# Left table factor of a long-convolution kernel: three products in one VectorE instruction, sums on TensorE

## The chip, the cores and the metric

The kernel runs on one core of one Trainium2 chip. The core has engines with a queue of instructions each, run in order: TensorE (PE, with its weight loads shown as PEld), VectorE (DVE), ScalarE (ACT), GpSimd (POOL) and SyncE (SP, which here only issues DMAs). [...] The metric is the device time of one execution in microseconds (us); lower is better.

## The reference, cut to what matters

Two branches read the same input `x` of 2048 positions by 512 channels, and a gate mixes them:

```python
g = _sigmoid((x * gate_w).sum(-1, keepdims=True))
a = _A_ref(x, A_re, A_im, B_re, B_im, C_re, C_im, log_dt, Dskip)
b = _B_ref(x, wqkv, w_phi, wo)
return g * a + (1 - g) * b
...
# _A_ref: a long convolution per channel d, by FFT
logdA = dt * A;  dB = dt * Bc                                  # complex, (512, 128)
P = jnp.exp(logdA[:, :, None] * l[None, None, :])              # l = 0..2047
K = jnp.einsum("dn,dnl,dn->dl", Cc, P, dB).real                # the convolution's kernel
y = irfft2(rfft2(pad(u)) * rfft2(pad(K)))[..., :L] + u * Dskip
...
# _B_ref: linear attention, 32 heads of 16
phi_k = concat(softmax(k @ w_phi), softmax(-k @ w_phi));  phi_q likewise
num = phi_q @ (phi_k^T v);  den = phi_q . sum(phi_k) + 1e-6;  o = (num / den) @ wo
```

What the change touches is `K`: for each channel a sum over 128 complex modes of C times dB times an exponential in the position `l`, of which the real part is kept.

## The kernel before, in words

**The table for K.** The 128 modes lie on the partitions. A position is split as l = 512a + 64b + t, with a in 0..3, b in 0..7 and 64 values of t. So the exponential is a product of three: the left factor is A(a,b) = C(a) times D(b), 32 complex values for each mode and channel, where the table `Ctab` (C) holds the term in a with C and dB folded in, and `Dtab` (D) holds the term in b; the right factor R(t) is made of a real exponential (`E`, stretched by `Gtab`) times a cosine and a sine (`cs`). K is the real part, so it is the sum over modes of Re(A) Re(R) and Im(A) Im(R) with signs put into the tables; TensorE does that sum with A as the 32 columns of weights and R as 64 moving columns, once per channel.

**Units.** The 512 channels go in 16 units U of 32. Units 0 to 7 take their C from the first half of the table (`C[0]`), 8 to 15 from the second (`C[1]`). In `kgen` each unit has on DVE: `A1` (L1037), which multiplies two planes of C by the first plane of D; `A2` (L1042), which multiplies two planes of C by the second plane of D (C has three planes, the third being the negative of the first); and for six units `A3` (L1047), which adds the two results. Each of these instructions writes 2048 bf16 values per partition. The table `FOURS` says for which ten units A3 is left out: TensorE then adds the four products itself (`kgen_chunk`, L209: four terms of 32 matmuls, 128 in all; with A3 two terms, 64 matmuls). `El` (L989), `Rh` (L1054) and `Rl` (L1058) make R. There is one buffer for A, so A1 of the next unit waits until the matmuls of this one are done.

**Stages.** Until about 99 us (`prepare`, `keys_and_spectrum`, `attention_keys`): loads, transposes of x, the forward transform of x (`XAu`, `xst`, written to `XUd`), the tables C, D, G, and the keys and values of the attention. There ACT makes exponentials of the keys (`Ek`), DVE sums them (`Zk`), and values are copied out of PSUM into one of two buffers `vb` and scaled (`vr`, L692). Then the units follow each other. Behind every four of them, 128 channels are transformed (`psA`, `XA`, `psB`, `XK`), multiplied with the spectrum of x (`t`, L1230), transformed back (`psz`, `Zr`, through DRAM as `Zd` and `ZT`, `psy`), gated (`xT<-psy`, L1330) and written out (L1341). The attention's queries are worked in between. The last four units go as groups (12, 13), (14) and (15), and the last one in halves (`KD`, `KDb`; `XA`, `XAb`).

**The order.** `Plan` records every step as a node with what it needs and the buffers it takes; `ORDER`, a string of node numbers, fixes in which order they are issued; `SIDES` says for each copy out of PSUM (L175 on ACT, L177 on DVE) and for some DMA issues on which engine it goes, and `RINGS` from which ring its PSUM buffer comes. Nothing is decided while it runs. A line such as L96 (ACT functions) or L347 (`tt`, DVE products of tables) belongs to a helper; the tile's name tells the step.

Of the kernel before, what the change touches and what calls it, by code (L numbers as in the profile page):

```python
# [98 lines left out]
class Plan:  # L99

    DIGITS = "0123456789abcdefghijklmnopqrstuvwxyzABCDEFGHIJKLMNOPQRSTUVWXYZ-_"
    ORDER = ("0001021d0x0y0z0o0p0q0G0H0I0f0g0h0D0E0F170i0j0k181415162z2C0304051h2E0l0m0n0607082F0u0v0w2D0r0s0t2G2I2K1e1f090a0b1C2H0c0d"
             "0e1g2M1A1i1j1k0A0B0C1r2L2N2O2J1D1s102P11121t131L0-1E1u1v1w2S1M0_1B2Q2T2R1N1F1I0Y2U1b0Z1G2V1J191a2W0J0K0L0M0N0O0P0Q0R0S0T"
             "0U0V0W0X1c1S2X4n202Y2Z4u4v4w2A2-4x4J2_304y4K4L4M31324B4F4z4A4C1H4N344G4D334Q4E4H4I4Y1P4R364O354Z4U371K4P1R4S4-4V4_533839"
             "542B4T504W1X1O571Y4X513a525b3C585c3c5d5e59555i3b5j563d5a5f5q5r5g3h5m1U5s3i5h5t5k5x3D5n3j5o5l5u5y3e3f3g5B5p1Z5F5v5C3k5w3o"
             "5H5z5G5D5M5A5I3q1T5E215J3E3p5Q1V5R5K4o5N5L5U1Q3r3l3m3n4p1l1m1n5O1x1y1z1-5W3v3x5V5S3y5P3F1W3w5X5T67693G4q683I5Y6a3H6b3J5Z"
             "3K6c3M1o1p1q5-6d3L3N3s3t3u3O1_235_3P223Q3R25243S3U3T2b272d3V263W2c3z3A3B2f3X2h2e28632j2i3Y3Z3-3_402g2l412k43442s2u482942"
             "2t2m4a2n4b2o454647492p4f2q4c4d4e2w2r2v4h2a2x6064612y4i4g656e874r6i628b6f6j4j4k4l6g6686858a6k4m6h6l886r6m7x898c4s8d8e6t6q"
             "8h8i4t8j8f8n8g6u7y8k8l8B8o8t8p6v6w6s8C6-8m6x8q6y8u6_70718r9_8Y8Z8-8H6z8s6A6B72748v8D7z8Ia06n6o6p756C736D9293948w8K8E8F6E"
             "8L8x8y6F6G6H768M8G8z778Q787B8A7C8J6I6J6K8Ra8796M6N6O7a7A8N8Oa97b9R8P8S9Va19W6Laaa26P9S8T7D9X7c7d7e9U9Z8U6Qa5a36Sa68W8Vae"  # L110
             "a48X9Ta79Y6Tam7f7g7h9-6U6Ranaf7i6W7Eabac98as8_9091ad996X9a7F9g7Gag6V7n7H9h7Iao7j7k7lbSah7JbT7patavaw9b9i7K9596977m9c9j9k"
             "7L7M7Nap9o9paBaxbI9w9x6YaibMbNajakbJaqal6Z9q7r7O7P7QbO7S7T7U7oar7qauaC7RbL7sbQay9y7t7Waz9l9m9naA7YbK7u7vaD7ZaPaQaR7VbPb_"
# [1479 lines left out]
```

## Time and profile before

| | |
|---|---|
| Time, median of 3 runs | 252.83 us (251.02 to 253.78) |
| The profiled execution's own time | 252.17 us |
| Its span on the core | 250.4 us |
| DVE busy | 224.2 us, 90% |
| ACT busy | 211.0 us, 84% |
| PE busy | 202.3 us, 81% |
| POOL busy | 2.4 us, 1% |

A profile is one execution. "Busy" is the time in which an engine executes an instruction. A group of instructions has a count, a total and the mean of one; since the next instruction of a queue starts a little before the last one's end is recorded, the distance from start to start is the better price of an instruction in a full queue. "Idle before" names how long the engine stood still ahead of a group and what ended that. The granted clock of TensorE was 1.00 in most of the span, and 0.52 between 75 and 90 us.

### The profile page before, as it was taken

The page shows a single profiled execution, that of the slowest core. Times are in us where ns is not written, and L with a number is a line of the kernel's source. Part 1 is how long each engine was busy: PE and PEld are TensorE (multiplying, and loading weights), DVE is VectorE, ACT ScalarE, POOL GpSimd, SP SyncE. Part 2 cuts the span into 40 slices and gives each one's busy share as a digit, 9 for nine tenths or more (in the row PEclk, how much of TensorE's full clock was granted, in tenths as well). Part 3 has the DMA queues.
Part 4 walks back from the last instruction along what each step waited for, and adds up shares of the span by engine and source line. Part 5 has one row for each costly group of instructions (what it writes and reads, how often), then busy time and mean ns, then how long its engine had stood idle before and what let it go on. Part 6 is the DMA issues. An engine that isn't in the chain of part 4 may idle for free.

```text
span 250.4 us, 9850 instructions
## 1 busy us (share of the span) xinstructions
PE 202.3 (81%) x4412; PEld 141.8 (57%) x4437; DVE 224.2 (90%) x287; ACT 211.0 (84%) x291; POOL 2.4 (1%) x7
## 2 busy tenths in 40 slices
PE   0695999999956468798797778889999789998970
PEld 0584755447734434256456646765777576877550
DVE  0388999989899988999999999999999999999680
ACT  2058999999999999999999999999999999974430
POOL 0200000000000000000000000000000000000000
PEclk9999999999995569999979999999999999999985
DMA  6999910236280477400619129804896879998664
GB/s 134 275 174 159 404 49 4 90 105 134 56 256 0 145 235 223 160 3 13 174 49 240 38 73 243 265 3 92 197 209 192 219 206 234 225 235 165 185 171 75
DMA packets 61922, 38.23 MB, mean 153 GB/s; under 512 B 40632, under 2 KB 57272, under 8 KB 61496
## 3 DMA queue, kind: packets, MB, share of 16 engines
q1 hardware_dynamic: 61880, 37.61, 60.0%
q8 instruction: 34, 0.56, 1.0%
q14 instruction: 8, 0.07, 0.1%
HBM read 24.49 MB, written 13.11 MB: 150 GB/s over the span
## 4 chain that ended last, share of the span: by engine, by line
PE 28%; DVE 24%; ACT 23%; DMA 10%; SPq 7%; issue 5%; ACTq 0%; DVEq 0%
ACT Eq L96 4%; PE pk L635 4%; ACT cs L96 4%; DMA UD<-in_A_u_dram 4%; PE vp L683 4%; SPq L1465 3%; ACT E L96 3%; PE kps L209 2%; DMA ZT<-Zd 2%; PE psB L542 2%; ACT XA L175 2%; ACT L93 2%; DVE t L1230 2%; PE psy L750 2%; PE psz L1256 2%
## 5 line engine op out<-in xcount | busy, mean ns | idle before, releaser
L209 PEld LDWEIGHTS <-A 128*32 128x32 bf16 x1664 | 28.5, 160 | 6.2 <-issue 3.6
L209 PE MATMUL kps<-R,A 128*32 128x64 bf16 x1664 | 30.3, 229 | 1.8 <-DVE A L1042 0.5
L96 ACT ACTIVATE cs<-args 128x1024 bf16<-128x1024 f32 x32 | 30.7, 1050 | 0.2 <-PE args L953 0.2
L1058 DVE TENSOR_TENSOR R<-E,cs 128x2048 bf16<-128x2048 bf16 x16 | 19.5, 1217 | 0.0
L1037 DVE TENSOR_TENSOR A<-Ctab,Dtab 128x2048 bf16<-128x2048 bf16 x16 | 19.5, 1217 | 0.0
L1054 DVE TENSOR_TENSOR R<-E,cs 128x2048 bf16<-128x2048 bf16 x16 | 19.5, 1217 | 0.0
L1042 DVE TENSOR_TENSOR A<-Ctab,Dtab 128x2048 bf16<-128x2048 bf16 x16 | 19.5, 1217 | 0.0
L175 ACT CAST Zr<-psz 128x1024 bf16<-128x1024 f32 (+1 forms) x17 | 16.5, 974 | 2.5 <-issue 1.2
L542 PE MATMUL psB<-XAu,TB 64*128 64x128 bf16 x256 | 12.8, 262 | 7.1 <-ACT xst L175 4.9
L175 ACT CAST XK<-psB 128x1024 bf16<-128x1024 f32 (+1 forms) x15 | 15.0, 1010 | 3.8 <-PE psB L222 2.3
L175 ACT CAST XA<-psA 128x1024 bf16<-128x1024 f32 (+1 forms) x16 | 15.6, 1002 | 3.2 <-PE psA L216 3.2
L683 PE MATMUL vp<-WW,xT 128*128 128x512 bf16 x59 | 16.9, 403 | 0.8 <-issue 0.7
L1230 DVE TENSOR_TENSOR t<-XUX,XK 128x2048 bf16<-128x2048 bf16 x14 | 17.0, 1218 | 0.5 <-ACT XK L175 0.5
L96 ACT ACTIVATE Ek<-pk 128x512 bf16<-128x512 f32 x32 | 16.8, 602 | 0.4 <-PE pk L635 0.2
L769 PE MATMUL pq<-xT,Wqp 128*128 128x512 bf16 x64 | 16.5, 396 | 0.6 <-ACT Eq L96 0.6
L96 ACT ACTIVATE Eq<-pq 128x512 bf16<-128x512 f32 (+1 forms) x28 | 16.7, 711 | 0.2 <-PE pq L769 0.2
L96 ACT ACTIVATE E<-args 128x1024 bf16<-128x1024 f32 x16 | 16.8, 1058 | 0.0
L542 PEld LDWEIGHTS <-TB 64*128 64x128 bf16 x256 | 10.3, 116 | 11.2 <-issue 11.0
L1256 PE MATMUL psz<-t,small 128*128 128x512 bf16 x49 | 14.6, 380 | 2.0 <-ACT cs L96 0.5
L635 PE MATMUL pk<-WW,xT 128*128 128x512 bf16 x57 | 15.5, 380 | 0.5 <-issue 0.2
L662 DVE TENSOR_REDUCE Zk<-Ek 128x64 f32<-128x1024 bf16 x12 | 14.0, 1209 | 0.0
L222 PE MATMUL psB<-XA,TB 128*128 128x128 bf16 (+2 forms) x160 | 9.6, 205 | 4.1 <-ACT XA L175 1.4
(178 smaller groups left out, 463.8 us busy)
## 6 DMA issues: line engine op xcount, KB each, us to landing
...
```

The source lines that it names most:

```text
L96: return self.nc.scalar.activation(**kw)
L175: self.nc.scalar.copy(out=o, in_=i)
L209: nc.tensor.matmul(kps[32 * dj:32 * dj + 32, g4, e, :], lhsT=A[:, ka, :, :, d].rearrange("p a b -> p (a b)"), rhs=R[:, kr, d, :], start=(i ...
L542: nc.tensor.matmul(box.ps[:, c2, sl, :], lhsT=fc.TB[rows, b0:b0 + 2].rearrange("p a b -> p (a b)"), rhs=X.t[rows, k, r0 + sl].rearrange("p ...
L635: nc.tensor.matmul(box.ps[:], lhsT=xT[:, st, kt, :], rhs=g.WW[:, kt, :], start=(kt == 0), stop=(kt == 3))
L683: nc.tensor.matmul(box.ps[:], lhsT=xT[:, st, kt, :], rhs=g.WW[:, 4 + kt, :], start=(kt == 0), stop=(kt == 3))
L1037: nc.vector.tensor_tensor(out=c.A[:, 0:2].rearrange("p o a b c -> p (o a) b c"), in0=g.C[U // 8][:, 0:2, :, d0 % 256:d0 % 256 + 32].rearra ...
L1042: nc.vector.tensor_tensor(out=c.A[:, 2:4].rearrange("p o a b c -> p (o a) b c"), in0=g.C[U // 8][:, 1:3, :, d0 % 256:d0 % 256 + 32].rearra ...
L1054: nc.vector.tensor_tensor(out=c.R[:, :, :, 32:64], in0=t.E[:, 1].unsqueeze(1).to_broadcast([128, 2, 32, 32]), in1=t.cs[:], op=ALU.mult)
L1058: nc.vector.tensor_tensor(out=c.R[:, :, :, 0:32], in0=t.E[:, 0].unsqueeze(1).to_broadcast([128, 2, 32, 32]), in1=t.cs[:, ::-1, :, ::-1], o ...
L1230: nc.vector.tensor_tensor(out=box.t, in0=Ls[r0 // ns].X[:], in1=box.XK[:].unsqueeze(1).to_broadcast([128, 2, 1024]), op=ALU.mult)
L1256: nc.tensor.matmul(box.ps[:, hb, :], lhsT=fc.TI[:, k].rearrange("p h a t -> p (h a t)"), rhs=box.t[:, k, 512 * hb:512 * hb + 512], start=( ...
```

## The change

A complex product can be had from three multiplications: with C = R + iI and D = d0 + i d1 (signs aside), the products (I - R) d0, (I + R) d1 and R (d0 - d1) are enough, since the last plus the second is R d0 + I d1 and the last plus the first is I d0 - R d1. The change does this as follows.

- The C table's three planes hold R, I - R and I + R. In `prepare` the sum over both planes (one instruction of 2048) and the sign flip (`p_cn`) of each half give way to four instructions of 1024: `p_cr`, `p_ci`, `p_cm`, `p_cp`.
- `Dtab` gets five planes and is laid out unit by unit: planes 0 and 1 (channels 0 to 255) and 3 and 4 (256 to 511) are d0 and d1, plane 2 is d0 - d1, made by one instruction of 2048 (`DS0` ahead of the first unit, `DS1` ahead of unit 8).
- A unit has one DVE instruction `A1` of 3072 in place of A1, A2 and A3, and always 128 matmuls: `kgen_chunk` adds two of the three products for each part.
- The value buffers `vb`, now four, lie in plane 2 of D; DS0 therefore waits for the last `vr`. `zrow` (the gate's row) lies in columns of `TB` that the forward transform is done with, and the small `rows` have a tile of their own.
- `ORDER`, `SIDES` and `RINGS` are other strings.

```diff
@@ class Plan @@
-    ORDER = ("0001021d0x0y0z0o0p0q0G0H0I0f0g0h0D0E0F170i0j0k181415162z2C0304051h2E0l0m0n0607082F0u0v0w2D0r0s0t2G2I2K1e1f090a0b1C2H0c0d"
...
+    ORDER = ("0l0m0n0001020x0y0z1h1e1d0304050607081C1A1D0o0p0q14151f0f0g0h160i0j0k1L0r0s0t0Y171i1g1r1s1t1M181T0G0H0I0-0D0E0F090a0b0c0d"
...
-    FOURS = ("0111111101011000")
...
-def kgen_chunk(nc, kps, A, R, four):
+def kgen_chunk(nc, kps, A, R, h):
 
+    terms = ((2, 0), (2, 1), (1, 0), (0, 1)) if h == 0 else ((0, 0), (0, 1), (2, 0), (1, 1))
     for e in range(2):
         for g4 in range(4):
-            terms = [(k, k) for k in range(2)] if not four else [(0, 0), (2, 0), (1, 1), (3, 1)]
...
-                                     rhs=R[:, kr, d, :], start=(i == 0), stop=(i == len(terms) - 1), tile_position=(0, 32 * dj), skip_group_check=True)
+                                     rhs=R[:, kr, d, :], start=(i == 0), stop=(i == 3), tile_position=(0, 32 * dj), skip_group_check=True)
...
@@ def prepare @@
-        V("p_px", lambda h=h: tt(C[h][:, 0:2], F.P[:], F.Q[:], ALU.add), r="t0 t1 t5 t6", w=f"Cn{h} Ci{h}")
-        V("p_cn", lambda h=h: nc.vector.tensor_scalar(out=C[h][:, 2], in0=C[h][:, 0], scalar1=-1.0, scalar2=None, op0=ALU.mult), r=f"Cn{h}", w=f"C{h}")
+        oR, oM, oP = (2, 0, 1) if h == 0 else (0, 1, 2)
+        V("p_cr", lambda h=h, oR=oR: tt(C[h][:, oR], F.P[:, 0], F.Q[:, 0], ALU.add), r="t0 t1 t5 t6", w=f"Cn{h} Ci{h} C{h}")
+        V("p_ci", lambda: tt(F.P[:, 1], F.P[:, 1], F.Q[:, 1], ALU.add), r="t0 t1", w="t5 t6")
+        V("p_cm", lambda h=h, oM=oM, oR=oR: tt(C[h][:, oM], F.P[:, 1], C[h][:, oR], ALU.subtract), r="t5 t6", w=f"C{h} Ci{h} Cn{h}")
+        V("p_cp", lambda h=h, oP=oP, oR=oR: tt(C[h][:, oP], F.P[:, 1], C[h][:, oR], ALU.add), r="t5 t6", w=f"C{h} Ci{h} Cn{h}")
...
@@ def attention_keys @@
             def cv(box=box):
-                box.v = g.kwk.tile([128, 16, 32], BF16, name="vb", bufs=g.P.k["vb"])
+                box.k = g.vfree.pop(0)
+                box.v = g.D[:, 2, 2 * box.k:2 * box.k + 2].rearrange("p u b c -> p (u b) c")
...
+    P.add("DVE", "DS0", lambda: nc.vector.tensor_tensor(out=g.D[:, 2], in0=g.D[:, 0], in1=g.D[:, 1], op=ALU.subtract), vs + [polar], rw=("", "DS"))
...
@@ def kgen @@
             def a1(c=c, d0=d0, U=U):
-                c.A = g.wk.tile([128, 4, 4, 8, 32], BF16, name="A", tag="A", bufs=g.P.k["A"])
-                nc.vector.tensor_tensor(out=c.A[:, 0:2].rearrange("p o a b c -> p (o a) b c"),
...
-            def a2(c=c, d0=d0, U=U):
...
-            def a3(c=c):
-                nc.vector.tensor_tensor(out=c.A[:, 0:2], in0=c.A[:, 0:2], in1=c.A[:, 2:4], op=ALU.add)
...
+                c.A = g.wk.tile([128, 3, 4, 8, 32], BF16, name="A", tag="A", bufs=g.P.k["A"])
+                h, c0 = U // 8, d0 % 256
+                nc.vector.tensor_tensor(out=c.A[:], in0=g.C[h][:, :, :, c0:c0 + 32].unsqueeze(3).to_broadcast([128, 3, 4, 8, 32]),
+                                        in1=g.D[:, 2 * h:2 * h + 3, U % 8].unsqueeze(2).to_broadcast([128, 3, 4, 8, 32]), op=ALU.mult)
+
+            if U == 8:
+                P.add("DVE", "DS1", lambda: nc.vector.tensor_tensor(out=g.D[:, 2], in0=g.D[:, 3], in1=g.D[:, 4], op=ALU.subtract), [sh], rw=(Dk, "DS"))
+            an = [P.add("DVE", "A1", a1, [sh], take=["A"], rw=(Ck + " " + Dk + " DS", ""))]
...
@@ def full_kernel @@
-        P = Plan(nc, {"XAu": 1, "UDp": 1, "xst": 2, "wT": 1, "Ek": 2, "Zk": 2, "vr": 2, "vb": 2, "acc": 1, "r8": 3, ...
+        P = Plan(nc, {"XAu": 1, "UDp": 1, "xst": 2, "wT": 1, "Ek": 2, "Zk": 2, "vr": 2, "vb": 4, "acc": 1, "r8": 3, ...
...
-        g.D = persist.tile([128, 2, 8, 512], BF16, name="Dtab")
+        g.D = persist.tile([128, 5, 8, 8, 32], BF16, name="Dtab")
```

How the order of DVE's queue changes where the units begin: before, from the attention's `KVbd` on (`zrow` and `SSw` belong to the gate and the attention, `zs` and `den` to its queries).

```order
L718 TENSOR_TENSOR KVbd<-kvp,small 32x8x32 x4
L721 TENSOR_TENSOR SSw<-small,zcol 128x8x8
L1037 TENSOR_TENSOR A<-Ctab_72,Dtab 128x2048
L1042 TENSOR_TENSOR A<-Ctab_72,Dtab 128x2048
L620 TENSOR_SCALAR zrow<-zps 128x512
L1047 TENSOR_TENSOR A<-A 128x2048
L989 TENSOR_TENSOR E<-E,Gtab 128x1024
L1054 TENSOR_TENSOR R<-E,cs 128x64x32
L1058 TENSOR_TENSOR R<-E,cs 128x64x32
```

And the same place of DVE's queue in the changed kernel (L734 is `DS0`, L1048 the wide A1).

```order
L726 TENSOR_TENSOR KVbd<-kvp,small 32x8x32 x4
L729 TENSOR_TENSOR SSw<-small,zcol 128x8x8
L734 TENSOR_TENSOR Dtab<-Dtab 128x2048
L1048 TENSOR_TENSOR A<-Ctab_71,Dtab 128x3072
L1057 TENSOR_TENSOR R<-E,cs 128x64x32
L1000 TENSOR_TENSOR E<-E,Gtab 128x1024
L1061 TENSOR_TENSOR R<-E,cs 128x64x32
```

DS0 has come in front of the first unit, and one instruction stands where three stood.

The end of DVE's queue before, from the copy of the last unit's K on (`KD`, L177; L1281 is a transpose of 32 by 32 blocks, L1330 the gating of a convolution's result, L913 that of the attention's alone):

```order
L177 CAST KD<-kps 128x256
L177 CAST KDb<-kps 128x256
L177 CAST xT<-bps 128x2x128
L177 CAST XAb<-psA 128x512
L1233 TENSOR_TENSOR t<-XUX,XK 128x2x512 x2
L177 CAST xT<-bps 128x2x128
L177 CAST XK<-psB 128x512
L1168 TENSOR_TENSOR t<-XUX,XK 128x2x512
L913 TENSOR_SCALAR xT<-bps,gT 128x384
L1168 TENSOR_TENSOR t<-XUX,XK 128x2x512
L1281 STREAM_TRANSPOSE ZS<-Zr 128x1024
L1330 TENSOR_TENSOR xT<-psy,gT 128x16x64
```

The same end of DVE's queue in the changed kernel (L1333 and L1331 are the gatings, L1284 the transpose):

```order
L175 CAST KD<-kps 128x256
L175 CAST KDb<-kps 128x256
L175 CAST XA<-psA 128x512
L1236 TENSOR_TENSOR t<-XUX,XK 128x2x512
L1333 TENSOR_TENSOR xT<-psy,gT 128x8x128
L1236 TENSOR_TENSOR t<-XUX,XK 128x2x512
L1171 TENSOR_TENSOR t<-XUX,XK 128x2x512
L1331 TENSOR_TENSOR xT<-psy,gT 128x4x128
L1171 TENSOR_TENSOR t<-XUX,XK 128x2x512
L175 CAST Zr<-psz 128x1024
L175 CAST Zr<-psz 128x32x16
L1284 STREAM_TRANSPOSE ZS<-Zr 128x1024
```

Behind these rows follow a third copy of `Zr` (128x32x16), a transpose and the four gatings of the last channels, the one of 16x64 now as the last of them, where it was the first. The gatings of 8x128 and 4x128, which stood just ahead of the KD rows before, now stand behind them; the three copies of `Zr` were ACT's; the copies of `bps` and one of `XK` have gone to ACT.

The end of SP's queue before, which holds only DMA issues:

```order
L1341 DMA out_dram<-xT 32x12x128 x2
L1290 DMA ZT<-Zd_0_118 32x2048 x4
L1341 DMA out_dram<-xT 32x12x128 x2
L1341 DMA out_dram<-xT 32x12x256 x4
L925 DMA out_dram<-xT 32x4x384 x4
L1341 DMA out_dram<-xT 512x1x64 x8
```

The end of ACT's queue in the changed kernel, which now holds the last eight writes (L1344), behind its last copies and gatings:

```order
L173 CAST xT<-bps 128x2x128
L922 ACTIVATE xT<-bps,gT 128x384 x2
L173 CAST xT<-bps 128x2x128
L922 ACTIVATE xT<-bps,gT 128x384
L1344 DMA out_dram<-xT 512x1x64 x8
```

SP's queue there ends with the four writes of 32x4x384, and the eight have moved from SP to ACT.

More of the change, by code (lines that the diff above doesn't have):

```diff
@@ L362, in prepare @@
     for b in range(8):
-        S("p_d", lambda b=b: act(out=g.D[:, 0, b, :], in_=are(), func=ACT.Exp, scale=64.0 * (b - 3.5)), r="act t2", w=f"D{b}")
+        S("p_d", lambda b=b: act(out=g.D[:, 0:4:3, :, b, :], in_=are().rearrange("p (h u c) -> p h u c", h=2, u=8), func=ACT.Exp, scale=64.0 * (b - 3.5)), r="act t2", w=f"D{b}")
     S("p_g", lambda: act(out=g.G[:], in_=are().unsqueeze(2).to_broadcast([128, 512, 2]), func=ACT.Exp, scale=-32.0), r="act t2", w="G")
@@ L619, in ge @@
     def ge():
-        nc.vector.tensor_scalar(out=g.zrow[:], in0=G.ps[:], scalar1=80.0, scalar2=-80.0, op0=ALU.min, op1=ALU.max)
+        nc.vector.tensor_scalar(out=g.zrow, in0=G.ps[:].rearrange("p b (k t) -> p b k t", k=4), scalar1=80.0, scalar2=-80.0, op0=ALU.min, op1=ALU.max)
         G.ps = None
     a2 = P.add("PE", "zps", gd, [b] + xt, take=["ps"], rw=("atm", ""))
-    g.gate.append(P.add("DVE", "g_z", ge, [a2], drop=["psum"]))
+    g.gate.append(P.add("DVE", "g_z", ge, [a2], drop=["psum"], rw=("", "TB0")))
     g.xTr = [a, a2]
-    kv = []
+    kv, vs, g.vfree = [], [], list(range(P.k["vb"]))
     for s2 in range(8):
@@ L805, in z2 @@
             nc.vector.tensor_tensor(out=Q.den[:, 0, :], in0=Q.den[:, 0, :], in1=Q.den[:, 1, :], op=ALU.add)
-            nc.vector.tensor_tensor(out=Q.z[:, 0:2, :], in0=Q.z[:, 0:2, :], in1=g.zrow[:, b:b + 1, :].to_broadcast([128, 2, 128]), op=ALU.add)
+            zk = Q.z[:, 0:2, :].rearrange("p s (k t) -> p s k t", k=4)
+            nc.vector.tensor_tensor(out=zk, in0=zk, in1=g.zrow[:, b].unsqueeze(1).to_broadcast([128, 2, 4, 32]), op=ALU.add)
         def z3():
@@ L1030, in kgen @@
             plan_exp(P, nc, g, psum, U, t, psq, [sh])
-            four = P.FOURS[U] == "1"
             c = Bag()
@@ L1401, in full_kernel @@
         g, fc, at = Bag(), Bag(), Bag()
[L1402 removed]
+        P = Plan(nc, {"XAu": 1, "UDp": 1, "xst": 2, "wT": 1, "Ek": 2, "Zk": 2, "vr": 2, "vb": 4, "acc": 1, "r8": 3, "ax": 1, "nrm": 1, "E": 2, "cs": 4, "A": 1, "R": 2,
                       "KD": 1, "XA0": 1, "XK": 2, "Zr": 2, "XUX": 3, "ln": 8}, {"ps": 2, "p0": 2, "bk": 3, "acc": 1, "pf": 2})
@@ L1437, in full_kernel @@
         g.ldc, g.gw, g.Dcol_b = g.vecs[:, 0:4], g.vecs[:, 4:8], g.vecs[:, 8:12]
-        g.rows = g.zrow[0:12, 0, 0:64].bitcast(BF16)
         ck = ExitStack()
@@ L1453, in full_kernel @@
         g.wc = g.up.tile([128, 4, 16], BF16, name="wc")
+        g.rows_t = g.up.tile([128, 128], BF16, name="rows")
+        g.rows = g.rows_t[0:12]
         g.oT = {}
@@ L1493, in shift @@
         def shift():
-            g.rawd = g.ld_b = g.up = g.xau = g.ptmp = g.wc = None
+            g.rows_t = g.rows = g.rawd = g.ld_b = g.up = g.xau = g.ptmp = g.wc = None
             cu.close()
```

78 lines of the change are left out of this document (36 added, 42 removed).

## The prediction

> **What bounds the kernel now.** I read the page's totals first, then the chain that ended last, and then windows of the trace cut where the kernel's stages change, because a mean over 250 us mixes stages with different limits.
>
> ```profile
> span 250.4 us, 9850 instructions
> ...
> PE 202.3 (81%) x4412; PEld 141.8 (57%) x4437; DVE 224.2 (90%) x287; ACT 211.0 (84%) x291; POOL 2.4 (1%) x7
> ...
> PE 28%; DVE 24%; ACT 23%; DMA 10%; SPq 7%; issue 5%; ACTq 0%; DVEq 0%
> ```
>
> No engine has the chain to itself. The windows (columns: stretch, length, then busy us and instructions of PE, PEld, DVE, ACT and POOL, granted clock, DMA share, GB/s) say where each of them counts.
>
> ```profile
> 24.80:93.70 68.90, 57.87 (x915) 37.09 (x928) 65.93 (x98) 65.19 (x106) 0.00 (x0) 0.88 0.44 134
> 99.20:228.60 129.40, 113.59 (x2858) 82.27 (x2870) 128.39 (x136) 123.57 (x159) 0.00 (x0) 0.99 0.60 153
> 177.00:190.00 13.00, 12.47 (x371) 9.56 (x370) 12.97 (x17) 12.40 (x17) 0.00 (x0) 1.00 0.80 180
> 228.60:250.40 21.80, 13.38 (x373) 8.55 (x364) 12.39 (x19) 6.21 (x10) 0.00 (x0) 0.82 0.64 153
> ```
>
> The second row is the stage of the units, which is what the change is about. DVE is idle for only 1.0 of its 129.4 us, so DVE is the bound there. ACT has 5.8 us of idle and PE 15.8 us. What DVE is spared shortens the stage only until PE, which gets more work, or ACT is full. In the best 13 us (third row) PE reached 12.47/13.00 = 96%, in the whole stage 88%. The last row is the tail, where no engine is full: there a longer chain counts in full.
>
> ```profile
> 99.22 1.22 DVE L1037 TENSOR_TENSOR A<-Ctab,Dtab 128x2048 bf16<-128x2048 bf16 x1
> ...
> 230.84 0.41 DVE L177 CAST KD<-kps 128x256 bf16<-128x256 f32 x1
> ```
>
> These two instructions cut the execution in three: 99.22 us up to the first A, 230.84 - 99.22 = 131.6 us for the stage up to the copy of the last unit's K, and the rest. The profiled execution took 252.17 us, 1.77 more than its span, and is 0.66 below the median of 252.83. The sum is made on 252.17, and I do not correct for the difference, which is far inside the scatter of the three runs.
>
> **Prices.** They are taken from start to start in a full DVE queue.
>
> ```profile
> 157.06 1.22 DVE L1037 TENSOR_TENSOR A<-Ctab,Dtab 128x2048 bf16<-128x2048 bf16 x1
> 158.20 1.22 DVE L1230 TENSOR_TENSOR t<-XUX,XK 128x2048 bf16<-128x2048 bf16 x1
> ...
> 160.47 0.68 DVE L177 CAST oT<-ops 128x512 bf16<-128x512 f32 x1
> 161.07 1.22 DVE L840 TENSOR_TENSOR Eq<-Eq,ax 128x2048 bf16<-128x2048 bf16 x1
> ...
> 163.93 0.68 DVE L989 TENSOR_TENSOR E<-E,Gtab 128x1024 bf16<-128x1024 bf16 x1
> 164.54 1.22 DVE L1037 TENSOR_TENSOR A<-Ctab,Dtab 128x2048 bf16<-128x2048 bf16 x1
> ```
>
> A product of 2048 costs 1.14 us (157.06 to 158.20), a product of 1024 costs 0.61, and a copy of 512 out of PSUM 0.60. From 1024 to 2048 the price rises by 0.53, so an instruction of 3072 should cost 1.14 + 0.53 = 1.67 us. No row shows that size. From below it is bounded by 1.14, and from above by 3 x 1.14 = 3.4, three of the old ones; I take the straight line because two points lie on it. Copies of 1024 out of PSUM last as long as products of 2048 and are priced like them:
>
> ```profile
> L177 DVE CAST xst<-psB 128x1024 bf16<-128x1024 f32 x6 | 7.3, 1218 | 0.4 <-PE psB L542 0.4
> L175 ACT CAST xst<-psB 128x1024 bf16<-128x1024 f32 x10 | 10.0, 1024 | 1.2 <-DMA XUd<-xst 0.9 <-PE psB L542 0.3
> ```
>
> **Up to the first A: +1.5 us.** In each of two halves a sum of 2048 and a sign flip give way to four instructions of 1024.
>
> ```profile
> 84.06 0.42 DVE L386 TENSOR_SCALAR Ctab<-Ctab 128x1024 bf16<-128x1024 bf16 x1
> 84.39 1.22 DVE L347 TENSOR_TENSOR ppx<-Ctab,pt 128x2048 bf16<-128x2048 bf16 x1
> ```
>
> That is 1.14 + 0.33 before and 4 x 0.61 after, +0.97 for a half and +1.9 for both. DS0 is one more product of 2048, +1.1, and stands directly ahead of the first A, so whatever it waits for holds the whole queue of units behind it. Against that one copy of `vb` (0.6) and a few small steps (1.0 together) stand earlier in the new order, where the first row of the windows leaves DVE 3.0 and ACT 3.7 us of idle in 68.9. The sum is +1.4, taken as +1.5. If the new order hides all of it in that idle it is 0; if DS0, which must wait for every value of the attention, also has to wait for ACT, it is +3.
>
> **The stage of the units on DVE: -11.0 us.**
>
> ```profile
> L1037 DVE TENSOR_TENSOR A<-Ctab,Dtab 128x2048 bf16<-128x2048 bf16 x16 | 19.5, 1217 | 0.0
> L1042 DVE TENSOR_TENSOR A<-Ctab,Dtab 128x2048 bf16<-128x2048 bf16 x16 | 19.5, 1217 | 0.0
> L1047 DVE TENSOR_TENSOR A<-A 128x2048 bf16<-128x2048 bf16 x6 | 7.3, 1217 | 0.0
> ```
>
> 38 instructions of 1.135 are 43.1 us; 16 of 1.67 are 26.7; so -16.4. DS1 gives back 1.1. Four copies of 1024 that were ACT's (one KD, two XA, one XK) cost 4 x 1.14 = 4.5, two of 512 (one wo, one table) 1.2, and the two small steps of the gate 0.3: +6.0. The gatings of 8x128 and 4x128 have gone behind the cut, 1.1 + 0.6 = -1.7. The stage would be 131.6 - 11.0 = 120.6 us if DVE stayed the bound. ACT loses those four copies at 1.02 at least, so it needs at most 123.57 x 131.6/129.4 - 4.1 = 121.6.
>
> **The same stage on PE: -8.0 us, and this is the term I take.** Six units go from 64 to 128 matmuls.
>
> ```profile
> 112.73 2.25 PE L209 MATMUL kps<-R,A 128*32 128x64 bf16 x128
> 114.91 1.04 PE L769 MATMUL pq<-xT,Wqp 128*128 128x512 bf16 x4
> ...
> 210.06 1.21 PE L209 MATMUL kps<-R,A 128*32 128x64 bf16 x64
> 211.20 1.04 PE L1256 MATMUL psz<-t,small 128*128 128x512 bf16 x3
> ```
>
> 128 take 2.18 us (17 ns each) and 64 take 1.14, so 6 x 1.04 = +6.2, with the other 0.3 allowed for starts. [...]
>
> Work that moves behind the cut on PE: two groups of 32 `psy` matmuls, 16 products with `wo`, and one eighth of the attention's `ops`.
>
> ```profile
> L1319 PE MATMUL psy<-ZT,TJ 64*32 64x128 bf16 (+1 forms) x256 | 4.4, 211 | 0.3 <-DMA ZT<-Zd 0.3
> L750 PE MATMUL psy<-wo,oT 128*128 128x128 bf16 x96 | 7.4, 219 | 0.0
> L859 PE MATMUL ops<-Eq,KVbd 128*128 128x256 bf16 x64 | 8.5, 274 | 0.0
> ```
>
> These are 2 x 0.55 + 1.2 + 1.1 = 3.4 us. PE had 113.6 us of work in the second window and, at the same 88%, 2.0 in the 2.2 us from its end to the cut. With +6.5 and -3.4 it has 118.7 us. At the 96% of its best stretch that takes 123.6 us, more than DVE's 120.6 and ACT's 121.6. So PE, not DVE, ends the stage: 131.6 - 123.6 = 8.0 us less. The ends are -11.0 (PE's rows contain slack, DVE stays the bound) and +2.8 (PE keeps all its idle, below).
>
> **The tail: +1.8 us.** Behind the cut DVE gets the two gatings (+1.7) and three copies of `Zr`, one of 1024 and two of 512 (1.1 + 1.2), and loses two copies of 256 (0.7) and one of 512 (0.6): +2.8, all laid on the path, although it need not all be. Then come the last writes.
>
> ```profile
> 243.80 0.42 DVE L1330 TENSOR_TENSOR xT<-psy,gT 128x256 bf16<-128x256 f32 x1 [0.50 <-PE psy L1319]
> ...
> 242.50 5.35 SPq L1341 DMA_DIRECT2D out_dram<-xT  x8
> ```
>
> SP issues eight writes in 5.35 us, 0.67 each, up to 247.85, and the last lands at the span's end, 2.5 us later. From the last gating's end (244.22) to the end are 6.2 us. After the change ACT issues them; the 16x64 gating is now the last, with four issues behind it: 4 x 0.67 + 2.5 = 5.2, so -1.0. What an issue costs ACT is not shown; twice SP's price would add 2.7, and nothing excludes a gain of the same 0.67 or so for each. I take SP's price because it is the only row. The sum is +2.8 - 1.0 = +1.8, with ends -1 and +4.5.
>
> **The sum.** 252.17 + 1.5 - 8.0 + 1.8 = 247.5 us.
>
> **Rivals.** First, PE has more slack than its busy row shows, and DVE stays the bound: -11.0 for -8.0 gives 244.5. The windows speak for it in that weight loads take only 82.27 of 129.40 us, 64%; against it, that PE waited little in its full stretches. [...] Chance 0.20.
>
> Second, the ends of the table and the tail both come out high (+3 and +4), or the stage gives only about half of its 8.0 because ACT, which has up to 121.6 us of work there between the same waits, stands still meanwhile: 250 to 255. Chance 0.20.
>
> Third, slower: PE becomes the bound and keeps its idle time. A has one buffer, so the next A1 waits until all 128 matmuls of the unit before are done, and DVE's copies of PSUM are queued behind that A1; PE then waits for those copies, as it waits for ACT's now:
>
> ```profile
> L222 PE MATMUL psB<-XA,TB 128*128 128x128 bf16 (+2 forms) x160 | 9.6, 205 | 4.1 <-ACT XA L175 1.4
> L953 PE MATMUL args<-selE,statC 64*128 64x512 bf16 x32 | 6.8, 404 | 3.9 <-ACT cs L96 1.7 <-ACT E L96 1.2 <-ACT XA L175 0.5
> ```
>
> With all 15.8 us of idle the stage would be 118.7 + 15.8 = 134.5, 2.9 longer than now, and the sum 252.17 + 1.5 + 2.9 + 1.8 = 258.4. It decides from the point where PE's idle stays above 131.6 - 118.7 - 3.3 = 9.6 us. Against it: those waits end by ACT, which is relieved. Chance 0.12.
>
> Fourth, the wide instruction, whose operands have one more dimension, loses DVE's rate and costs three times 1.14 = 3.4: 16 x 1.7 = 28 more on DVE, some 273 us. Against it, another instruction that reads its operands in short runs keeps the rate:
>
> ```profile
> L1058 DVE TENSOR_TENSOR R<-E,cs 128x2048 bf16<-128x2048 bf16 x16 | 19.5, 1217 | 0.0
> ```
>
> Chance 0.03.
>
> **How the numbers follow.** The forecast has 0.45: PE at about 96% in the stage, 247.5 us. Two runs of this kernel differ by up to 1%, so about 1% is what a measurement can tell from no change; that is 250.3 to 255.4. Below it lie the first rival and nearly all of the forecast, 0.64; within it the second, 0.21; above it the third and fourth, 0.15. The range leaves out those two and a little on either side: from 243.0, the first rival with 1.5 less for table section or tail, to 254.5, nearly the end of the second.
>
> **What would show it.** The A group has 16 instructions of about 1750 ns and DVE's busy total falls to about 214 us; `kps` has 2048 matmuls. The first A starts near 100.7 us and the KD copy near 224.3. Between them PE's idle falls to about 5 us, and DVE has 3 us of idle, most of it ahead of A or a copy and ended by PE. ACT's queue issues the last eight writes. If the A group's mean is above 2 us, the price of 3072 was wrong; if the stage is near 121 us, the first rival holds; if PE's idle there is above 10 us, the third; and if the stage is right but the end is not, the table section or the tail was mis-sized.

## The result: slower by 5.1%

The changed kernel takes 265.13 us (median of 4 runs, 265.09 to 267.16) against 252.96 us of the kernel before (251.02 to 253.78). The ratio is 1.051, with a 95% interval of 1.044 to 1.059: 12 us slower, where 247.5 us were forecast. Its profiled execution took 265.09 us, with a span of 263.4 us on the core. Some executions of a kernel run longer at a lower clock (in experiment 5 three of 269.9 to 271.1 us at a mean granted clock of 0.93, against one of 265.5 at 0.94): the ratios leave them out, and since the profiled executions of experiments 5, 6 and 13 were of that kind, places in their traces are read, and no conclusion rests on their times alone.

The page of the changed kernel, the lines that answer to those of before:

```profile
span 263.4 us, 10603 instructions
...
PE 209.0 (79%) x4801; PEld 148.5 (56%) x4821; DVE 216.1 (82%) x274; ACT 208.0 (79%) x288; POOL 2.7 (1%) x7
...
ACT 40%; PE 28%; DVE 14%; issue 10%; DMA 3%; SPq 1%; ACTq 0%; DVEq 0%
```

DVE lost 8.1 us of work (about 10 were forecast), and ACT 3.0. "issue", time in which an engine waited for nothing that the profile shows, has doubled from 5% to 10% of the chain that ended last. The same cuts as in the prediction, by windows of the changed kernel (stage of the units; a hole; the rest of the tail; the last writes), and the tail of the kernel before:

```profile
99.90:230.70 130.80, 116.60 (x3202) 85.32 (x3209) 119.87 (x122) 115.86 (x149) 0.00 (x0) 0.98 0.56 145
230.70:236.10 5.40, 0.70 (x25) 0.62 (x26) 0.76 (x2) 0.00 (x0) 0.00 (x0) 0.85 0.92 149
236.10:255.40 19.30, 17.47 (x382) 12.23 (x382) 12.90 (x17) 6.45 (x11) 0.00 (x0) 0.85 0.31 75
255.40:263.40 8.00, 0.00 (x0) 0.00 (x0) 0.00 (x0) 0.00 (x0) 0.00 (x0) 0.50 0.74 168
```

```profile
230.80:244.30 13.50, 11.43 (x277) 6.87 (x277) 10.69 (x18) 4.68 (x8) 0.00 (x0) 0.94 0.67 181
```

Three things are to be seen. The stage is as long as before (130.8 for 131.6 us), although DVE has 10 us less to do: its idle time has grown from 1.5 to 11 us, and ACT's from 6.5 to 15. Then PE stands still for 4.7 of 5.4 us while the DMA engines are 92% busy, and behind that the granted clock is at half for some 5 us. And the tail behind that hole is still 19 us where it was 13.5. The clock from 236 to 241 us (the number before the DMA engines' share is their row's granted clock) and then the timelines of PE and of DVE:

```profile
236.00:241.00 5.00, 4.87 (x81) 4.46 (x81) 2.51 (x4) 1.60 (x2) 0.00 (x0) 0.50 0.50 107
```

```profile
230.61 0.79 PE L220 MATMUL psB<-XA,TB 128*128 128x32 bf16 x25
236.13 0.35 PE L220 MATMUL psB<-XA,TB 128*128 128x32 bf16 x7 [4.73 <-issue]
```

```profile
230.73 0.42 DVE L175 CAST KD<-kps 128x256 bf16<-128x256 f32 x1 [2.85 <-PE kps L207]
231.07 0.41 DVE L175 CAST KDb<-kps 128x256 bf16<-128x256 f32 x1
238.49 0.69 DVE L175 CAST XA<-psA 128x512 bf16<-128x512 f32 x1 [7.00 <-PE psA L214]
```

The wide instruction and the matmuls cost what was worked out for them (groups of the changed kernel):

```profile
L207 PE MATMUL kps<-R,A 128*32 128x64 bf16 x2048 | 36.5, 230 | 5.4 <-issue 3.6
L1048 DVE TENSOR_TENSOR A<-Ctab,Dtab 128x3072 bf16<-128x3072 bf16 x16 | 28.0, 1751 | 3.7 <-PE kps L207 3.7
```

| piece of the span | before | after | moved | forecast |
|---|---|---|---|---|
| up to the first A | 99.22 | 99.87 | +0.7 | +1.5 |
| first A to the copy of KD | 131.6 | 130.9 | -0.8 | -8.0 |
| KD to the end of the last gating | 13.4 | 24.6 | +11.2 | +2.8 |
| the last writes | 6.2 | 8.1 | +1.9 | -1.0 |
| span | 250.4 | 263.4 | +13.0 | -4.7 |

So two questions: why did the stage not get shorter, and what made the tail longer?

### The profile page after: what moved, and what is told of

It reads as the page before. It is cut to its first block, busy times and chain, and to the rows that moved or that the text cites. A ratio compares the mean times of both kernels' runs of the same rounds, so it can differ in the third digit from the quotient of the medians.

```text
span 263.4 us, 10603 instructions
## 1 busy us (share of the span) xinstructions
PE 209.0 (79%) x4801; PEld 148.5 (56%) x4821; DVE 216.1 (82%) x274; ACT 208.0 (79%) x288; POOL 2.7 (1%) x7
## 4 chain that ended last, share of the span: by engine, by line
ACT 40%; PE 28%; DVE 14%; issue 10%; DMA 3%; SPq 1%; ACTq 0%; DVEq 0%
ACT Ek L96 4%; PE kps L207 4%; ACT cs L96 4%; ACT xst L173 4%; ACT XAu L173 3%; PE pq L779 3%; PE psy L760 2%; DVE R L1057 2%; ACT trg L96 2%; ACT E L96 2%; DVE R L1061 2%; PE psz L1259 2%; PE psy L1322 2%; ACT XK L173 2%; DVE A L1048 2%
## 5 line engine op out<-in xcount | busy, mean ns | idle before, releaser
L207 PE MATMUL kps<-R,A 128*32 128x64 bf16 x2048 | 36.5, 230 | 5.4 <-issue 3.6
L207 PEld LDWEIGHTS <-A 128*32 128x32 bf16 x2048 | 34.6, 161 | 9.7 <-issue 5.9
L1048 DVE TENSOR_TENSOR A<-Ctab,Dtab 128x3072 bf16<-128x3072 bf16 x16 | 28.0, 1751 | 3.7 <-PE kps L207 3.7
L1057 DVE TENSOR_TENSOR R<-E,cs 128x2048 bf16<-128x2048 bf16 x16 | 19.4, 1218 | 1.4 <-ACT E L96 1.4
L1061 DVE TENSOR_TENSOR R<-E,cs 128x2048 bf16<-128x2048 bf16 x16 | 19.4, 1219 | 0.2
L688 PE MATMUL vp<-WW,xT 128*128 128x512 bf16 x61 | 15.8, 392 | 0.5 <-issue 0.5
L547 PE MATMUL psB<-XAu,TB 64*128 64x128 bf16 x256 | 11.2, 244 | 5.3 <-ACT xst L173 2.7
L173 ACT CAST Zr<-psz 128x1024 bf16<-128x1024 f32 x14 | 14.2, 1044 | 1.4 <-PE psz L1259 1.2
L173 ACT CAST XA<-psA 128x1024 bf16<-128x1024 f32 x13 | 13.1, 1032 | 2.0 <-PE psA L214 1.9
L640 PE MATMUL pk<-WW,xT 128*128 128x512 bf16 x57 | 14.3, 379 | 0.5 <-issue 0.2
L547 PEld LDWEIGHTS <-TB 64*128 64x128 bf16 x256 | 9.3, 108 | 8.9 <-issue 8.9
L173 ACT CAST xst<-psB 128x1024 bf16<-128x1024 f32 x14 | 14.0, 1030 | 0.2 <-PE psB L547 0.2
```

The lines of the kernel that those rows point to most:

```text
L173: self.nc.scalar.copy(out=o, in_=i)
L207: nc.tensor.matmul(kps[32 * dj:32 * dj + 32, g4, e, :], lhsT=A[:, ka, :, :, d].rearrange("p a b -> p (a b)"), rhs=R[:, kr, d, :], start=(i ...
L547: nc.tensor.matmul(box.ps[:, c2, sl, :], lhsT=fc.TB[rows, b0:b0 + 2].rearrange("p a b -> p (a b)"), rhs=X.t[rows, k, r0 + sl].rearrange("p ...
L640: nc.tensor.matmul(box.ps[:], lhsT=xT[:, st, kt, :], rhs=g.WW[:, kt, :], start=(kt == 0), stop=(kt == 3))
L688: nc.tensor.matmul(box.ps[:], lhsT=xT[:, st, kt, :], rhs=g.WW[:, 4 + kt, :], start=(kt == 0), stop=(kt == 3))
L1048: nc.vector.tensor_tensor(out=c.A[:], in0=g.C[h][:, :, :, c0:c0 + 32].unsqueeze(3).to_broadcast([128, 3, 4, 8, 32]), in1=g.D[:, 2 * h:2 * ...
```

## The experiments

Every kernel is cut at its own first A and KD. "Stage" is the length from the first A to KD in its profiled execution, and "tail" the length from KD to the end of the last gating; the expectations count some tails to the end of the span, with the last writes.

**1. The arithmetic in the old order.** The changed kernel with `ORDER`, `SIDES` and `RINGS` of the kernel before:

```
-    ORDER = ("0l0m0n0001020x0y0z1h1e1d...      # as changed
+    ORDER = (the nodes in the order of the kernel before; A1 where A1 was; p_cr, p_ci, p_cm, p_cp where p_px was; DS0, DS1 ahead of A1 of units 0 and 8)
```

> The changed arithmetic (wide A1, five-plane D, new C tables, always 128 matmuls) in the issue order, engine sides and PSUM rings of the kernel before; the wide A1 stands where A1 stood, A2 and A3 are gone, DS0 and DS1 stand directly ahead of the first A1 that needs them. PE theory (TensorE with its waits has become the bound of the stage of the units, whatever the order): the stage stays at 129 to 134 us, and with the tail of the kernel before the time is 251 to 256 us. Order theory (the new order loses what the arithmetic gains): the stage falls to 121 to 126 us and the time to 243 to 249 us. Either way the tail behind the copy of KD is back at 18 to 21 us from 32.7.

Measured: 264.82 us, ratio 1.054 [1.045, 1.062]. The tail is back at 14.7 us (20.2 with the last writes, as expected), but the stage has grown to 141.9 us, 10 more than before. Neither theory had that. The new order alone is thus not what costs the 12 us: with the old one the same arithmetic costs as much, in another place.

**2. The last inverse transforms behind the last unit.** On PE `psy` of the third quarter goes behind `psB` and `psz` of the last unit (`psBh` and `opsL` are the halves of its `psB` and the last `ops`, `pya` is the attention's part of `psy`):

```
 psA psBh opsL psBh psz      # the last unit
+psy128 pya psy128           # third quarter, stood ahead of psA (first) and behind opsL, psBh
```

> The changed kernel with one thing in its order moved: on TensorE the two inverse transforms (psy) of the third quarter of the channels, which need the last load of ZT but one, stand behind the transforms of the last unit's K (psA, psB, psz) instead of ahead of them; their gatings on VectorE and their writes follow. Theory of the tail (TensorE's 4.7 us standstill at 231.4 us is the wait for that load, and everything of the last unit queues behind it): 4 to 6 us less than the changed kernel, 259 to 261 us. Rival (the tail is set by the DMA traffic, the Zd and ZT transfers and the last writes, and the standstill only fills time): less than 1 us of change, 264 to 266 us.

Measured: 267.67 us, ratio 1.069, slower still. The hole was not the wait for that load: `psA` stands right behind `psB` now, and the hole is there all the same, 3.9 us at the same matmul.

```profile
229.90 0.79 PE L220 MATMUL psB<-XA,TB 128*128 128x32 bf16 x25
234.61 0.35 PE L220 MATMUL psB<-XA,TB 128*128 128x32 bf16 x7 [3.92 <-issue]
```

My theory of the tail fell with this, and I looked for what these standstills have in common. In several kernels they lie a multiple of 256 PE instructions apart, matmuls and weight loads counted alike (in the changed kernel 767, 2045, 1276 and 510 recorded instructions lie between the standstills that end at 138.1, 157.7, 196.9, 222.9 and 236.1 us, which is 3, 8, 5 and 2 times 256 less one to four, and a trace can lack a few records); and the trace has packets on an instruction queue of its own (queue, packets, MB, share of the DMA engines' time; the page of the changed kernel):

```profile
q8 instruction: 37, 0.61, 1.0%
```

These are 16 KB each, and PE's 9622 matmuls and weight loads on 37 packets are 260 a packet, as are the 8849 on 34 packets of the kernel before. From here on the theory is: PE's program comes in pages of 256 instructions, and PE stands still where it has run through a page before the next has arrived.

**3. More matmuls, less VectorE, in the kernel before.**

```
-    FOURS = ("0111111101011000")
+    FOURS = ("1111111111111111")
```

> The kernel before with the table FOURS all ones: the six A3 additions are gone from VectorE (6 x 1.14 = 6.8 us) and six units go from 64 to 128 matmuls on TensorE (+6.5 us), in the order of the kernel before. Theory that VectorE bounds the stage and TensorE's idle time can be filled: 4 to 7 us faster, 246 to 249 us. PE theory (TensorE with its waits is as much the bound): within 2 us of the kernel before, 251 to 255 us, with VectorE idle by 4 to 7 us more.

Measured: 265.4 us, ratio 1.055 [1.050, 1.060]. One string in the kernel before, which takes 6.8 us from DVE and adds 6.5 us to PE by the prices of the prediction, gives a loss of the same size. It lies in the stage, 143.2 us, where that of the changed kernel lies in the tail. So in the old order what matters is the 384 additional matmuls, and their price is near twice their time.

**4. Half of the products on TensorE.** In the changed kernel:

```
-            for i, (ka, kr) in enumerate(terms):
+            for i, (ka, kr) in enumerate(terms[:2]):
```

> The changed kernel with only two of the four products of each part of K computed on TensorE (64 matmuls for a unit instead of 128, 1024 fewer, 17 us); the other two are left out, so K is not complete. PE theory: the stage from the first A to the copy of KD falls by 6 to 11 us from 130.8, to where VectorE is full (120 to 125 us). Rival (the stage is held by waits of the order between ScalarE and VectorE, not by TensorE's work): it stays above 128 us. The tail keeps its standstill.

Measured: 258.24 us (one run). The stage is 128.1 us, only 2.8 less, for 17 us less matmul time by the price of one (11 us less busy time). The hole in `psB` is gone, against what was expected: PE stands still for 1.1 us at a later place (236 us), and the tail is 18.9 us.

**5. The whole program shifted by half a page.**

```
                 box.ps = psum([128, 4, 256], "psA")
+                for i in range(64 if h == 1 and g4 == 7 else 0):
+                    nc.tensor.matmul(box.ps[0:32, 0, 0:64], lhsT=..., rhs=..., start=True, stop=True, ...)
```

> The changed kernel with 64 additional small matmuls (32 weight columns, 64 moving columns, 128 instructions with their weight loads, about 1.1 us) on TensorE in an idle stretch at about 73.4 us, where they write PSUM that the next matmuls overwrite. They only shift everything behind them by half of 256 instructions in TensorE's program. Fetch theory (TensorE stands still at every 256th instruction when the next 16 KB of its program has not arrived): at the five places where it stood still without a named cause (138.1, 157.7, 196.9, 222.9 and 231.4 us, 10.0 us together) it runs through, and the standstills, if any, come 64 matmuls earlier or later; the time changes by more than 1.5 us in either direction from 265.1. Rival (these standstills are waits for data that the profile does not name): the same five places, about 10 us together, and 265 to 266.5 us.

Measured: 270.31 us median, 265.49 to 271.14, without a ratio. Only places are read from it: `psB` of the last unit runs through, and PE stands still in other places, all half a page from the old ones: at 183, 192, 198 and 232 us, and for 2.5 us up to 239 us, between the 89th and the 90th of the last unit's 128 matmuls. The hole has moved, and is not gone.

**6. The last writes on SyncE again.**

```
 # SIDES of the four "out" nodes of the last channels
-ACT
+SP
```

> The changed kernel with its last eight output writes issued by SyncE again instead of ScalarE; nothing else. Theory (SyncE's remaining writes stood from 247.96 to 255.79 us because they waited for a write that ScalarE issued at 253.55 us): SyncE writes the others before, and 2 to 4 us are gained, 261 to 263.5 us. Rival (the end is set by the last gating and the transfer behind it, whoever issues): 264.5 to 266 us.

Measured: 264.37 us, ratio 1.048 [1.039, 1.058] against 1.051 of the changed kernel: at most a microsecond, less than expected. What was expected is what the changed kernel's waits of SP's queue and its timeline show:

```profile
SPq L1344 <- DMA out_dram<-xT: 8.2, 2, 7.8
```

```profile
253.55 5.86 ACTq L1344 DMA_DIRECT2D out_dram<-xT  x8
254.09 1.22 DVE L1333 TENSOR_TENSOR xT<-psy,gT 128x1024 bf16<-128x1024 f32 x1 [0.62 <-PE psy L1322]
255.79 1.56 SPq L1344 DMA_DIRECT2D out_dram<-xT  x3
257.44 2.79 SPq L936 DMA_DIRECT2D out_dram<-xT  x4
```

SP's remaining seven writes did wait until 255.79 for a write of ACT's queue. Without that wait the writes behind the last gating are 7.3 us here, and 7.0 in experiment 14, instead of 8.1.

**7. The old number of matmuls with the new arithmetic.** As experiment 1, but the six units with an A3 get one addition behind the wide A1 and 64 matmuls:

```
+    terms = terms if four else terms[2:]
...
+                if "0111111101011000"[U] == "0":      # both others += the shared product, 2048
+                    nc.vector.tensor_tensor(out=o, in0=o, in1=k.unsqueeze(1).to_broadcast([128, 2, 1024]), op=ALU.add)
```

> The changed arithmetic in the issue order of the kernel before (as the first of the experiments), but the six units that had an A3 addition before have one again, directly behind the wide A1 (one VectorE instruction of 2048 that adds the shared product to both others), and 64 matmuls instead of 128. So TensorE has exactly the matmuls of the kernel before, and VectorE 16 x (2.27 - 1.67) = 9.6 us less for A, against 3.0 more for the tables. TensorE theory (what costs are the 384 additional matmuls, by their time and by their share of the program): 246 to 253 us. Rival (what costs is the wide instruction with one buffer for A, or the new tables): 259 us or more.

Measured: 254.40 us, ratio 1.011 [1.007, 1.016], 1.4 us above the range of TensorE's theory and well below the rival's 259. The matmuls of the units are those of the kernel before; what differs is DVE's arithmetic, with its tables. Windows of the stage:

```profile
101.86:233.56 131.70, 112.48 (x2923) 83.42 (x2934) 123.04 (x123) 122.82 (x158) 0.00 (x0) 1.00 0.58 150
```

DVE is busy for 123.0 us instead of 130.1, and the stage is 131.7 instead of 131.6. PE and ACT are 2 to 3 us less busy in this window too (112.5 for 115.5 and 122.8 for 125.1), since more of their work lies before the later first A (2923 matmuls in the window for 2942), and still the stage is no shorter. Seven microseconds taken from the engine that was idle for only 1.5 us are worth nothing.

**8. The time of the matmuls without their instructions.** In the kernel before:

```
-            an.append(P.add("DVE", "A3", (lambda: None) if four else a3, an[-1:]))
+            an.append(P.add("DVE", "A3", lambda: None, an[-1:]))
...
+                for _ in range(0 if four else 5):       # 512 columns each, overwritten
+                    nc.tensor.matmul(K.ps[:, cc]..., lhsT=g.ident[:], rhs=c.R[:, 0, 0:8, :]..., start=True, stop=True, ...)
```

> The kernel before; in the six units with an A3 addition that addition is left out, the 64 matmuls stay, and five matmuls of 512 columns (5 x 0.215 = 1.08 us) stand ahead of them, which write PSUM that is overwritten. Two of four products are missing from K in these units. So TensorE has the time of 128 matmuls in each unit, but 110 instructions less for each of the six. Theory of time alone (TensorE's time is the price): like the kernel with FOURS all ones, 263 to 267 us. Fetch theory (about half of the price of that kernel came from the length of TensorE's program): 253 to 259 us.

Measured: 258.64 us, ratio 1.027 [1.020, 1.034]. Windows of the stage, of this kernel and of experiment 3:

```profile
98.90:237.02 138.12, 120.76 (x2969) 86.15 (x2981) 124.22 (x132) 125.19 (x160) 0.00 (x0) 1.00 0.57 147
```

```profile
100.02:243.17 143.15, 120.91 (x3326) 89.87 (x3335) 124.36 (x132) 125.29 (x160) 0.00 (x0) 1.00 0.55 142
```

PE, DVE and ACT are busy for the same time in both, to 0.2 us. The time of the first, 258.64 us, is in the range of the fetch theory. Its stage is 6.5 us longer than before, about what was added to PE (6.5 us by the price of a matmul; the busy time rose by 5.2, from 115.5); that of the other is 5.0 us longer again, for the same busy time in some 700 instructions more. These are the two prices of the 384 matmuls in this order: their time, and their number; what the second consists of is read behind experiment 13.

**9 to 11. One engine relieved at a time, and all.** In the changed kernel; with experiment 4 these are PE, DVE, ACT and the three together.

```
+                nc.vector.tensor_tensor(out=c.A[:, 0:2], ...      # 9: two products of three
+        act(out=T.E[:, 1, 0:16], in_=box.ps[:, 0], func=ACT.Exp)  # 10: half of E; DVE reads it twice
 # 11: both of these and terms[:2]
```

> The changed kernel with A1 at 2048 instead of 3072 (two of the three products; the third is left out and TensorE reads another in its place, so K is wrong), 16 x 0.53 = 8.5 us less on VectorE, TensorE unchanged. Theory that VectorE's queue holds the stage of the units: 130.9 us falls by 5 to 8 us. Theory of coupling (each engine waits for the others in turn, and none of them alone is the bound): it falls by 0 to 3 us.

> The changed kernel with the exponentials E on ScalarE made for half of the channels only (16 instructions of 512 instead of 1024, about 7 us less on ScalarE); VectorE reads that half twice, so K is wrong for the other half, and its instructions keep their size. Theory that ScalarE's queue holds the stage of the units: 130.9 us falls by 5 to 7 us. Theory of coupling: it falls by 0 to 3 us.

> The changed kernel with all three reliefs at once: half of the products on TensorE (17 us and 2048 instructions less), A1 at 2048 (8.5 us less on VectorE) and half of E (7 us less on ScalarE); K is wrong. Theory of coupling: together they shorten the stage by more than the three apart, by 9 us or more, to below 122 us. Theory that a transfer or another wait outside these three engines sets the stage: above 125 us.

Measured: 265.7 us (ratio 1.055), 266.97 us (1.060) and 251.8 us (1.000). Windows of the stage: PE relieved (experiment 4), DVE, ACT, all.

```profile
101.52:229.62 128.10, 105.30 (x2179) 72.80 (x2187) 119.97 (x123) 115.14 (x149) 0.00 (x0) 0.93 0.56 146
```

```profile
100.05:230.95 130.90, 116.77 (x3212) 85.53 (x3210) 112.00 (x123) 116.03 (x149) 0.00 (x0) 0.99 0.56 145
```

```profile
100.56:232.42 131.86, 117.81 (x3212) 85.49 (x3211) 119.88 (x122) 109.87 (x149) 0.00 (x0) 0.97 0.56 144
```

```profile
101.09:222.17 121.08, 103.01 (x2183) 71.11 (x2183) 111.32 (x123) 108.97 (x149) 0.00 (x0) 0.94 0.59 152
```

11 us less on PE shorten the stage of 130.9 us by 2.8; 8 us less on DVE by nothing; 6 us less on ACT by nothing (+1.0); all three together by 9.8, where the sum of the three is 1.8. So no engine alone is the bound of this stage. They take turns, and each relief alone turns into idle time of the engine relieved.

**12. Fewer matmuls still, in the old order.** As experiment 7 with ten units instead of six:

```
-"0111111101011000"[U]
+"0101101100010000"[U]
```

> The order of the kernel before with the changed arithmetic, and ten units (0, 2, 5, 8, 9, 10, 12 to 15) instead of six with the addition on VectorE and 64 matmuls: against the kernel with six, four units less with 128 matmuls (4 x 1.04 = 4.2 us and 512 instructions less on TensorE) and 4.5 us more on VectorE, which had 8.7 us idle in that stage. TensorE theory (in that order its time, and its program's length, set the stage): 4 to 7 us less, 247 to 251 us. Coupling with ScalarE and VectorE: 252 to 256 us.

Measured: 258.02 us, ratio 1.026 [1.018, 1.033]. A miss. The stage is 134.5 us, 2.8 longer than with six, although PE's busy time is 2.0 us less (4 units of 64 matmuls, nominally 4 us) and DVE had 8.7 us of idle for the 4.6 us it got (123.0 to 127.6). More PE time cost about its full length in that order (experiment 8), but less of it was worth nothing here.

**13 and 14. Only the last pages shifted.** In the changed kernel 64 small matmuls at 208.7 us, and the same with SP's last writes:

```
         box.ps = psum([128, 2, 16, 32], "args")
+        for _ in range(64 if U == 15 else 0):
+            nc.tensor.matmul(box.ps[0:32, 0, 0:2]..., lhsT=g.ident[:, 0:32], rhs=..., start=True, stop=True, ...)
```

> The changed kernel with 64 additional small matmuls (128 instructions, 1.1 us) on TensorE at about 208.7 us, ahead of the last unit's arguments and into PSUM that these overwrite. Behind them every boundary of 256 instructions comes 64 matmuls earlier or later than before; ahead of them nothing changes. Fetch theory (the 4.7 us standstill at 231.4 us is the wait for a page of TensorE's program whose fetch was queued behind the data transfers of 226 to 236 us): the boundary now falls into the last unit's matmuls, its page is asked for at about 225 us, when the transfers are light, and the standstill is under 1.5 us; the tail behind the copy of KD is 19 to 21.5 us instead of 24.6, and with 1.1 us for the matmuls the time is 260 to 263 us. Rival (the standstill is a wait for data): it stays above 4 us at the same matmuls of psB, and the time is 265 to 267 us.

> The same, and the last eight output writes issued by SyncE instead of ScalarE. If SyncE's wait for ScalarE's writes costs anything at the end, it shows once the standstill is gone: 1 to 2.5 us less than the same kernel with ScalarE issuing, 258 to 261.5 us. If not: within 0.5 us of it.

Measured: 266.66 us (ratio 1.051 [1.037, 1.064]) and 265.74 us (1.059 [1.048, 1.071]); both times lie above what was expected (260 to 263 and 258 to 261.5). In place the theory of pages is right. The standstill has left `psB`, and comes where the boundary now lies, between the 89th and the 90th of the last unit's 128 matmuls (timeline of PE, of the first kernel and then of the second):

```profile
231.75 1.63 PE L207 MATMUL kps<-R,A 128*32 128x64 bf16 x89
237.28 0.86 PE L207 MATMUL kps<-R,A 128*32 128x64 bf16 x39 [3.90 <-issue]
238.07 1.03 PE L220 MATMUL psB<-XA,TB 128*128 128x32 bf16 x32
```

```profile
230.50 1.64 PE L207 MATMUL kps<-R,A 128*32 128x64 bf16 x89
233.32 0.80 PE L207 MATMUL kps<-R,A 128*32 128x64 bf16 x39 [1.18 <-issue]
```

In size it was wrong: 3.9 us here and 1.2 in the other, not under 1.5 in both, because the page did not come at 225 us, a stretch that was not quiet either (DMA engines 67% busy from 225 to 231 us): its packet ran from 234.77 to 235.98 us, behind PE's crossing of the boundary before it at 228.9. All places of the first kernel from 130 us to the end of the gatings where PE stood still for over a microsecond, from the records of PE and of the instruction packets (the profile puts five of the six down to "issue", and the one at 196.44 to the copy of another unit's KD on DVE):

```
PE goes on at   stood still   PE instructions before it   last instruction packet landed
136.91 us       1.75 us        4289 = 16 x 256 + 193       135.43 us
157.29          2.11           5057 = 19 x 256 + 193       155.91
196.44          1.02           7105 = 27 x 256 + 193       194.53
213.58          1.39           7873 = 30 x 256 + 193       211.89
228.88          1.23           8641 = 33 x 256 + 193       227.43
237.28          3.90           8897 = 34 x 256 + 193       235.98
```

Every one is at the same place of a page, and ends 1.3 to 1.9 us after a packet of 16,384 bytes has landed.

The time did not follow, though: neither kernel is faster than the changed one. In the second the standstill fell from 4.7 to 1.2 us, with another of 1.2 us at 239.2 us, and stage and tail together are 155.5 us as in the changed kernel (155.4); the 1.1 us of added matmuls and a 1.3 us standstill at 212.9 us took part of it, and the granted clock was 0.50 from 236 to 241 us there too, and 0.60 from 241 to 246.

The same reading of the other traces tells what the second price in experiment 8 is. PE's standstills of over 0.2 us at that place of a page (to within the few records that a trace lacks), each ended 1.1 to 2.1 us after a packet had landed, are in the stage together:

```
kernel before                        1.4 us
experiment 8 (time alone)            1.3
experiment 7 (old number, new A)     1.5
experiment 3 (all with 128)          6.9
experiment 1 (changed, old order)    7.3
changed kernel                       5.6, and 4.7 in the tail
experiment 4 (half of the products)  0.4, and 1.1 in the tail
```

Experiments 3 and 8 differ by 5.6 us in these standstills and by 5.0 us in the stage. In the changed order they count for less: experiment 4 lost 5.2 us of them and 11 us of busy time, and its stage got 2.8 us shorter.

No run of these beats the kernel before. The nearest that computes the same is experiment 7, at 1.011.

## Why the prediction was wrong

**Prices.** These held. The wide A1 has a mean of 1751 ns (1750 forecast) and costs 28.0 us in all; DVE's busy total fell to 216.1 us (about 214); `kps` has 2048 matmuls; the first A starts at 99.87 us, 0.8 earlier than forecast. The price of 17 ns for a matmul of `kps` held too: 128 of them take 2.24 us in the changed kernel, and 2.18 from start to start (228.43 to 230.61 us).

**"The stage of the units": -8.0 forecast, -0.8 measured. This step failed first.** It took DVE for the bound because it was idle for only 1.0 us, let the next fullest engine take over at 96% of its time, and took the longest of the three engines' sums, 123.6 us, for the stage's length. Experiment 7 shows that DVE was full but not the bound: 7 us less left the stage where it was. Experiments 4, 9, 10 and 11 show the same of each engine in the changed kernel. PE reached 96% in one stretch of 13 us; over the stage it stayed at 116.6/130.8 = 89%, as before (88%). The third rival, that PE keeps its idle time, came nearest here: 14.2 us of idle against its 15.8, 130.9 us against its 134.5. It gave the A buffer as the mechanism; that wait (A1 behind `kps`) is 3.7 us in the changed kernel and 7 in experiment 1, but relieving DVE behind it (experiment 9) gained nothing, so it is a link of the chain and not its cause. A second buffer for A was not tried, so this part of the third rival stays open.

**The price of 384 matmuls: +6.5 forecast, counted only as PE's busy time.** In the old order it is 6.5 for their time plus 5.0 for their number in the stage (experiments 3 and 8), and 5.6 us more of standstills at page ends are found there. That a unit's 128 matmuls with their weight loads are 256 instructions, a whole page in 2.2 us, was nowhere in the sum. The rows of before held a hint: idle time of PE before `kps` and `psB` put down to "issue", 0.2 and 0.5 us, which I passed over.

**The tail: +2.8 forecast, +11.2 measured.** This term was too small, and left out the hole. In experiments 4 and 11 the tail has standstills of only 1.1 and 1.5 us, and is 18.9 and 19.4 us: without them about 17.8 in both, 4.4 more than before, which is the new order; in experiment 4 the granted clock was 1.00 from 225 to 246 us. Of the remaining 6.8 us the hole is 4.7; the other 2 are what is left for the half clock, an estimate by difference. That the hole is the late page is shown by its place (13, 14); how much time would be gained without it isn't, since the runs that shortened it lost as much elsewhere.

**The last writes: -1.0 forecast, +1.9 measured.** The price of an issue on ACT was right (5.86 us for eight, 0.73 each, for 0.67 taken); that SP's remaining writes would wait for ACT's was not seen. Undoing it gave about 1 us of that last stretch (7.3 and 7.0 for 8.1 us), of the 2.9 by which the term was off; the rest is not explained.

**The other rivals.** The first (DVE bound throughout, 244.5) is refuted by 7 and 9. The low share of the weight loads spoke for it, but did not show that PE had time to spare: in experiment 8 PE's added time passed into the stage about one to one (6.5 us) with weight loads at 86.2 of 138.1 us, 62%. The second (250 to 255) had the right sign of the tail and too small a size. The fourth (the wide instruction at a third of the rate) is refuted by the 1751 ns.

**What stays open.** What in detail ties the three engines in the stage, so that an addition to PE counts in full in the old order and no single relief does; the old order also got longer when PE lost 2 us and DVE gained 4.6 (experiment 12). What the changed order does with the old number of matmuls was not run. And why 2.6 us more pass before the first A in the old order with the new tables (101.86 in experiment 7).
